# Half-tile causal diagonal in chunked attention A, with value copies moved to the DMA queue

## The chip, the cores and the metric

The kernel runs on one core of a Trainium2 chip. The metric is the device time of one execution in microseconds (us); lower is better. Three runs of the kernel before took 351.57, 351.86 and 356.25 us, so the median is 351.86 us. The engines are called PE (matmul), PEld (its weight loads), DVE (vector), ACT (activation), POOL (GpSimd) and SP (the engine whose queue issues nearly all DMAs).

## The reference, cut to what matters

Two independent attentions are computed from two inputs of 2,048 tokens by 640 columns, with 32 heads of 20 columns each, and their outputs are set side by side.

```
# A: four segments of 512 tokens, causal softmax in a segment, a memory over the earlier ones
for s in range(4):
    logits = einsum('bhqd,bhkd->bhqk', qs, ks) * scale + mask      # mask: key > query
    a_dot = einsum('bhqk,bhkd->bhqd', softmax(logits), vs)
    a_mem = (phi(qs) @ M) / (phi(qs) @ z + 1e-06)
    o = g * a_mem + (1.0 - g) * a_dot                              # g = sigmoid(beta)
    M, z = M + phi(ks).T @ vs, z + sum(phi(ks))
# B: causal attention in a sliding window of 256
mask = (i - j >= 0) & (i - j < 256)
o = softmax(where(mask, q @ k.T * scale, -1e9)) @ v
out = concatenate([A's o @ wo, B's o @ wo], axis=-1)
```

## The kernel before, in words

**Tiling.** Each attention is cut into four chunks of 512 tokens, which run alternately: A0, B0, A1, B1, A2, B2, A3, B3. The 32 heads are eight groups of four. The four heads of a group lie on partitions 0, 32, 64 and 96, so that four small matmuls run side by side on the PE. For each chunk there are projections of q and k (five pieces of 128 columns) and of v (two halves of 16 heads), then scores, exponentials, masks, products with the values ("AV"), a transpose and a division, and an output projection. Three of the eight groups of q and k get their rows through a DRAM round trip of DMAs (`regroup`, lines 393 to 414).

**Scores.** `score_batch` (line 621) fills two PSUM tiles of 1,024 columns, one for each pair of heads of a group, with keys on the partitions and queries on the columns. One ACT instruction (line 647) takes the exponential of each tile into an SBUF tile `pt`. `mask` (line 658) then zeroes what the causal rule forbids: for A always on POOL, with `affine_select` (line 682); for B on POOL, and on DVE (line 664, a product with a constant 0/1 tile) for batches made of 64 by 64 corner blocks. `batches` (line 916) lists the batches of all chunks. In A, key tile `kt` of 128 keys is scored against all queries from `128*kt` on, and the 128 by 128 block on the diagonal is then masked: 512 + 384 + 256 + 128 = 1,280 columns a head. A batch has 512 columns a head, so two groups take five batches, and a chunk takes 20.

**AV.** `av` (line 687) multiplies the values of each key tile with the `pt` columns. In the last chunk, B3, `av_tile` (line 705) does it by query tile. `norm` (line 753) turns the result into `o`: a DVE transpose (`turn`, line 748), a reciprocal, and a product on POOL (line 782). For the memory term of A it first adds epsilon (line 768, DVE). `final` (line 812) stores `o` to DRAM, loads it back transposed (`oT`, line 835, two buffers), and `final_job` (line 843) multiplies it with `wo`, a row tile of 128 tokens by ten matmuls. While scores remain these use the two PSUM banks `m`, with two DVE copies (line 891) a row tile. Once the last score batch has been issued they use the score banks `sc`, with one ACT (line 874) or DVE (line 878) copy a row tile.

**Values.** `v_job` (line 550) writes the value tiles `vA` or `vB`. For B, `v_ends` (line 583) copies pieces of them on DVE (line 601) into `vL`, `vU` and `vX`, in which the rows that a corner block doesn't use are zero.

**Order.** Nothing is scheduled by the hardware. A planner (`Flow`, line 58, and the loop in `body`, from line 1116) keeps an estimated clock for each engine while it emits instructions. It issues a score batch when its inputs and a PSUM tile should be ready, otherwise an AV group, otherwise a step of a waiting projection; output projections come last in its list. Each engine runs its own queue strictly in the order that comes out. The costs given to `on_dve`, `on_pool`, `on_act` and `on_dma` steer this order and aren't instructions.

Of the kernel before, what the change touches and what calls it, by code (L numbers as in the profile page):

```python
# [9 lines left out]
ALU = mybir.AluOpType  # L10
BF16 = mybir.dt.bfloat16
F32 = mybir.dt.float32

P = 128
# [22 lines left out]
SH = P // 2  # L37
XC = SH + L

BANKS_A = [([(0, 0, 4, 0)], [("diag", 0, 1)]),  # L40
           ([(3, 3, 1, 0), (1, 1, 3, 128)], [("diag", 0, 2)])]
HALF = (2, 2, 2)

STRETCH = 10240.0 / 3.0
IDLE = 300.0
# [139 lines left out]
class _K:  # L185
# [140 lines left out]
    def consts_ends(self):  # L326
# [11 lines left out]
        nc.gpsimd.tensor_tensor(out=ends[:], in0=cm[:, 0, :], in1=cm[:, 1, :], op=ALU.add)  # L338
        self.ends = ends

    def load_beta(self, beta):
# [208 lines left out]
    def v_job(self, n, half, w_ap, v, gate, needs):  # L550
        nc, f = self.nc, self.f
        for need in needs:
            yield need
        xT = self.xs[n]
        x0 = SH if gate else 0
        for tt in range(LT):
            yield "bank"
            ps, bi = self.bank()
            for kt in range(self.KT):
                self.wide(ps, xT[:, kt, x0 + tt * P:x0 + (tt + 1) * P],  # L560
                          w_ap[:, half, kt, :], 320, kt == 0, kt == self.KT - 1)
# [12 lines left out]
            self.close(bi, f.on_dve(402.0, f.seen))  # L574
            f.open = False
        if not gate:
            self.v_ends(n, self.chunks[n][1], half, v)
        else:
            for g in range(4 * half, 4 * half + 4):
                self.mark(f.dve + 138.0, n, "v", g)  # L580
        self.used_x(n)

    def v_ends(self, n, c, half, v):


# [4 lines left out]
        todo = []  # L590
        if half == 0 and c > 0:
            pv = self.vB[(c - 1) % 2]
            todo += [(self.vU[hi, 0:2, :], pv[hi, 2:4, :], 580.0),
                     (self.vX[lo, :], pv[lo, 0, :], 380.0)]
        todo += [(self.vL[lo, :, s], v[lo, :, s], 610.0),
                 (self.vU[hi, 2:4, s], v[hi, 0:2, s], 320.0),
                 (self.vX[hi, s], v[hi, 0, s], 430.0)]
        left = [len(todo)]
        for out, in_, ns in todo:
            def go(out=out, in_=in_, ns=ns):  # L600
                self.nc.vector.tensor_copy(out=out, in_=in_)
                t = f.on_dve(ns)
                left[0] -= 1
                if left[0] == 0:
                    for g in range(4 * half, 4 * half + 4):
                        self.mark(t, n, "v", g)
# [14 lines left out]
    def score_batch(self, n, ent, kof, q, masks):  # L621

        nc, f = self.nc, self.f
        ps = [self.ps.tile([P, 2, 512], F32, name="sc", bufs=NSC) for _ in range(2)]
        cols = 0
        for g, ref, q0, nq, c0 in ent:
            k, kc = kof(ref)
            h0, h1 = {"a": (0, P), "f": (0, P), "l": (0, SH), "u": (SH, P)}[ref[0]]
            for j in range(4):
                rows = slice(HD * j, HD * j + DH)  # L630
                nc.tensor.matmul(ps[j // 2][h0:h1, j % 2, c0:c0 + nq],  # L631
                                 lhsT=k[rows, g, kc + h0:kc + h1],
                                 rhs=q[rows, g, q0:q0 + nq],
                                 start=True, stop=True, tile_position=(HD * j, h0),
                                 skip_group_check=ref[0] in "lu")
            cols += nq
        if ent[0][1][0] in "lu":
            t = f.on_pe("row64", 40.0 * len(ent), cols / 2)
        else:
            t = f.on_pe("row", cols / 2.4 + 10.0 * len(ent), cols)  # L640
        lo = min(e[4] for e in ent)
        hi = max(e[4] + e[3] for e in ent)
        pts = []
        ready = []
        for i in range(2):
            pt, slot = self.piece("pt", NPT, 1, BF16, (P, 2, 512))
            nc.scalar.activation(out=pt[:, :, lo:hi], in_=ps[i][:, :, lo:hi], func=ACT.Exp,  # L647
                                 scale=self.scale)
            te = f.on_act(2 * (hi - lo) * 0.833 + 52.0, t)
            self.sc_free.append(te)  # L650
            for m in masks:
                ready.append(None)
                self.mask(m, pt, te, ready, len(ready) - 1)
            pts.append(pt)
            self.pt_of.setdefault(n, []).append(slot)
        return pts, ready

    def mask(self, m, pt, te, ready, x):
        nc, f = self.nc, self.f
        kind, c0, n = m  # L660
        if kind == "ends":
            def go():
                blk = pt[:].rearrange("p h (b c) -> p (h b) c", c=SH)
                nc.vector.tensor_tensor(  # L664
                    out=blk, in0=blk,
                    in1=self.ends[:].unsqueeze(1).to_broadcast([P, 1024 // SH, SH]),
                    op=ALU.mult)
                ready[x] = f.on_dve(602.0, te)
            f.at(te - 50.0, go)
            return  # L670
        if kind == "diag":
            blk = pt[:, :, c0:c0 + n * P]
            pat = [[0, 2 * n], [1, P]]
            base, mul, r = 0, -1, 2 * n * P
        else:
            blk = pt[:].rearrange("p h (b c) -> p h b c", c=2 * P)[:, :, 0:n, c0:c0 + SH]
            sign = 1 if kind == "near" else -1
            pat = [[0, 2], [0, n], [sign, SH]]
            base, mul, r = (SH, -1, 2 * n * SH) if kind == "near" else (-1, 1, 2 * n * SH)

        def select():
            nc.gpsimd.affine_select(out=blk, in_=blk, pattern=pat, compare_op=ALU.is_ge,  # L682
# [70 lines left out]
    def norm(self, turned, dst, add_to, last, g=None):  # L753
# [11 lines left out]

        def s1():
            if add_to:
                nc.vector.tensor_tensor(out=rr[:], in0=tv[:, :, DH],
                                        in1=self.eps[:, g:g + 1].to_broadcast([P, NB]),
                                        op=ALU.add)  # L770
# [145 lines left out]
    def batches(self, chunks):  # L916
# [6 lines left out]
        far = lambda n: ("far", P + SH, n)  # L923
        for n, (kind, c) in enumerate(chunks):
            if kind == "A":
                for g0 in range(0, G, 2):
                    for g in (g0, g0 + 1):
                        for ent, ms in BANKS_A:
                            out.append([n, [(g, ("a", kt), P * q0, P * nq, c0)
                                            for kt, q0, nq, c0 in ent], ms, []])  # L930
                        if g == g0:
                            kt, q0, nq = HALF
                            out.append([n, [(g0 + x, ("a", kt), P * q0, P * nq, 256 * x)
                                            for x in range(2)],
                                        [("diag", 0, 1), ("diag", 256, 1)], [g0]])
                    out[-1][3].append(g0 + 1)
                continue

            def ends(g, qt, c0):
# [76 lines left out]
    def body(self, xA, A_wq, A_wk, A_wv, A_wo, A_beta, xB, B_wqkv, B_wo, out2d):  # L1016
# [38 lines left out]
        self.vU = big.tile([P, LT, VW], BF16, name="vU")  # L1055
        self.vX = big.tile([P, VW], BF16, name="vX")
        self.vA = self.v_tile("vA")
        self.consts_mz()
        nc.vector.memset(self.vL[:].bitcast(F32), 0.0)
        self.consts_mem()  # L1060
# [165 lines left out]
    def one_group(self, n, kind, c, g, what, parts, left, o_t, groups_done, scro, wo, out2d):  # L1226
# [135 lines left out]
```

## Time and profile before

The profiled execution took 352.71 us as a whole, of which the profile's span covers 350.6 us.

| engine | busy us | share of the span | instructions |
|---|---|---|---|
| PE | 326.4 | 93% | 5617 |
| ACT | 315.0 | 90% | 358 |
| POOL | 294.3 | 84% | 592 |
| DVE | 278.2 | 79% | 557 |

| part of the span | length us | what ends it |
|---|---|---|
| first score of A0 to first score of B0 | 46.2 | from 9.3 to 55.5 us |
| A1 and A2 and A3, each to the next chunk's first score | 37.3, 36.6, 36.8 | 132.7, 213.4, 291.8 us |
| B0, B1 and B2, each to the next chunk's first score | 39.9, 44.1, 41.6 | 95.4, 176.8, 255.0 us |
| B3, first to last score | 37.8 | 329.6 us |
| rest after the last score | 21.0 | 350.6 us |

The bounds are the start times of the score matmuls on PE in the trace. Busy time counts an engine as busy while any of its instructions runs. Matmuls are pipelined, so PE's share overstates its work; the times from the start of one matmul to the start of the next tell more. The granted PE clock was 1.00 throughout.

### The profile page before, as it was taken

What the parts mean: (1) busy time and instruction counts of PE and PEld (TensorE: products, weight loads), DVE (VectorE), ACT (ScalarE), POOL (GpSimd) and SP (SyncE); (2) the same over time, 40 slices, a digit from 0 to 9 for tenths busy, and PEclk for the clock granted to TensorE, in tenths of its full rate; (3) what the DMA queues carried; (4) which work ended last, traced back from release to release, by engine and by line L of the source; (5) the groups of instructions that cost most, each with busy time, mean ns of one, the idle gap of its engine ahead of it and who ended that gap; (6) DMA issues with size and microseconds to landing.
All of it is one profiled execution on the core that took longest, in us unless ns stands there. A gap on an engine that the chain in (4) does not pass through costs nothing.

```text
span 350.6 us, 13578 instructions
## 1 busy us (share of the span) xinstructions
PE 326.4 (93%) x5617; PEld 167.0 (48%) x5617; DVE 278.2 (79%) x557; ACT 315.0 (90%) x358; POOL 294.3 (84%) x592
## 2 busy tenths in 40 slices
PE   7999999989999999999999999988999999899994
PEld 2443435444544345455644436454543445566672
DVE  5687677999958999999967998997867999766621
ACT  2897499999999999999999999999999999989831
POOL 6589388988898989999898989899988989987720
PEclk9999999999999999999999999999999999999999
DMA  7945617526675133033794025030483032675773
GB/s 233 376 159 129 165 32 227 128 64 178 200 124 123 22 77 122 2 93 69 175 193 104 0 63 155 3 79 8 82 143 77 2 75 61 146 140 150 146 183 115
DMA packets 69374, 40.54 MB, mean 116 GB/s; under 512 B 48448, under 2 KB 67520, under 8 KB 69312
## 3 DMA queue, kind: packets, MB, share of 16 engines
q1 hardware_dynamic: 67584, 38.35, 45.2%
q10 hardware_dynamic: 1728, 1.32, 1.2%
q8 instruction: 44, 0.72, 0.9%
q14 instruction: 18, 0.15, 0.1%
HBM read 16.06 MB, written 16.38 MB: 93 GB/s over the span
## 4 chain that ended last, share of the span: by engine, by line
PE 48%; DVE 22%; POOL 11%; issue 6%; ACT 5%; DMA 5%; SPq 2%; DVEq 0%; ACTq 0%; POOLq 0%
PE m L735 30%; PE sc L631 9%; POOL pt L682 7%; PE m L696 6%; ACT pt L647 5%; DVE tt L748 4%; DVE pt L664 3%; DMA xT<-in_B_x_dram 2%; PE m L717 2%; DMA scr_o<-o 2%; POOL o L782 2%; DVE kB L445 1%; PE sc L735 1%; DVE pq L471 1%; DVE qA L445 1%
## 5 line engine op out<-in xcount | busy, mean ns | idle before, releaser
L647 ACT ACTIVATE pt<-sc 128x1024 bf16<-128x1024 f32 (+1 forms) x320 | 296.6, 1070 | 14.9 <-PE sc L631 12.9
L682 POOL TENSOR_SCALAR_AFFINE_SELECT pt<-pt 128x256 bf16<-128x256 bf16 x448 | 209.6, 495 | 36.0 <-ACT pt L647 30.8
L748 DVE STREAM_TRANSPOSE tt<-m 128x512 f32<-128x512 f32 x88 | 60.7, 706 | 19.4 <-PE m L696 9.4
L782 POOL TENSOR_TENSOR o<-tt,rr 128x320 bf16<-128x320 f32 x64 | 51.2, 801 | 2.8 <-DVE rr L774 2.7
L631 PE MATMUL sc<-qB,kB 20*64 20x64 bf16 (+2 forms) x1728 | 39.0, 217 | 1.2 <-issue 0.6
L735 PEld LDWEIGHTS <-xT 128*128 128x128 bf16 x320 | 28.7, 97 | 22.4 <-issue 11.6
L735 PEld LDWEIGHTS <-oT 128*128 128x128 bf16 x320 | 28.8, 97 | 17.2 <-issue 3.5
L631 PE MATMUL sc<-qA,kA 20*128 20x128 bf16 (+3 forms) x512 | 36.1, 300 | 0.9 <-ACT pt L647 0.3
L631 PEld LDWEIGHTS <-kB 20*64 20x64 bf16 (+1 forms) x1728 | 21.7, 98 | 25.1 <-issue 23.1
L735 PE MATMUL m<-wv_A,xT 128*128 128x320 bf16 x160 | 27.4, 300 | 3.7 <-DVE kA L445 2.0
L891 DVE CAST ot<-m 128x320 bf16<-128x320 f32 x46 | 21.9, 480 | 8.5 <-PE m L735 8.3
L735 PE MATMUL m<-xT,wq_A 128*128 128x512 bf16 x100 | 26.6, 386 | 1.1 <-DVE qA L445 0.9
L664 DVE TENSOR_TENSOR pt<-pt,ends 128x1024 bf16<-128x1024 bf16 x32 | 27.6, 875 | 0.0
L735 PE MATMUL m<-xT,wk_A 128*128 128x512 bf16 x100 | 27.2, 392 | 0.3
L735 PE MATMUL m<-xT,wBq 128*128 128x512 bf16 x100 | 25.8, 380 | 1.2 <-DVE tt L748 1.2
L735 PE MATMUL m<-xT,wBk 128*128 128x512 bf16 x100 | 25.3, 381 | 0.6 <-DVE kB L445 0.6
L735 PE MATMUL m<-wBv,xT 128*128 128x320 bf16 x160 | 25.6, 300 | 0.3 <-DVE tt L748 0.2
L631 PEld LDWEIGHTS <-kA 20*128 20x128 bf16 x512 | 10.5, 91 | 30.5 <-issue 29.8
L696 PE MATMUL m<-pt,vA 128*32 128x128 bf16 (+3 forms) x512 | 24.0, 302 | 0.5 <-POOL pt L682 0.3
L735 PE MATMUL m<-wo_A,oT 128*128 128x320 bf16 x120 | 20.8, 300 | 0.2 <-DVE ot L891 0.2
L802 POOL TENSOR_TENSOR o<-o,u 128x320 bf16<-128x320 bf16 x24 | 20.5, 854 | 0.0
L445 DVE CAST qB<-m 128x512 bf16<-128x512 f32 x20 | 13.6, 682 | 7.4 <-PE m L735 7.4
(87 smaller groups left out, 427.7 us busy)
## 6 DMA issues: line engine op xcount, KB each, us to landing
scr_o<-o SPq DMA_DIRECT2D x28, 160.0 KB
out_dram<-ot SPq DMA_DIRECT2D x27, 160.0 KB
xT<-in_B_x_dram SPq DMA_DIRECT2D x4, 720.0 KB
scr_pk<-e SPq DMA_DIRECT2D x15, 128.0 KB
xT<-in_A_x_dram SPq DMA_DIRECT2D x3, 640.0 KB
scr_kA<-kA SPq DMA_DIRECT2D x16, 60.0 KB
scr_qA<-qA SPq DMA_DIRECT2D x16, 60.0 KB
kA<-scr_kA SPq DMA_DIRECT2D x16, 60.0 KB
```

The lines of the kernel that those rows point to most:

```text
L445: nc.vector.tensor_copy(out=dst[:, m, at:at + L], in_=ps[:, :])
L631: nc.tensor.matmul(ps[j // 2][h0:h1, j % 2, c0:c0 + nq], lhsT=k[rows, g, kc + h0:kc + h1], rhs=q[rows, g, q0:q0 + nq], start=True, stop=Tr ...
L647: nc.scalar.activation(out=pt[:, :, lo:hi], in_=ps[i][:, :, lo:hi], func=ACT.Exp, scale=self.scale)
L664: nc.vector.tensor_tensor(out=blk, in0=blk, in1=self.ends[:].unsqueeze(1).to_broadcast([P, 1024 // SH, SH]), op=ALU.mult)
L682: nc.gpsimd.affine_select(out=blk, in_=blk, pattern=pat, compare_op=ALU.is_ge, fill=self.zero, base=base, channel_multiplier=mul)
L696: nc.tensor.matmul(O[HD * j:HD * j + HD, q0:q0 + nq], lhsT=v[:, VS * h:VS * h + HD], rhs=pts[j // 2][:, j % 2, c0:c0 + nq], start=(n_ == 0 ...
L717: nc.tensor.matmul(O[HD * j:HD * j + HD, o0:o0 + nq], lhsT=v[:, VS * h:VS * h + HD], rhs=pts[j // 2][:, j % 2, c0:c0 + nq], start=(n_ == 0 ...
L735: self.nc.tensor.matmul(ps[:, 0:n], lhsT=lhsT, rhs=rhs, start=start, stop=stop)
L748: self.nc.vector.transpose(out=tt[:], in_=O[:, :])
L782: nc.gpsimd.tensor_tensor(out=dst, in0=a, in1=b, op=ALU.mult)
L802: nc.gpsimd.tensor_tensor(out=dst, in0=dst, in1=u[:], op=ALU.add)
L891: nc.vector.tensor_copy(out=ot[:, 320 * hf:320 * hf + 320], in_=ps[:, 0:320])
```

## The change

**Diagonal.** A key tile is now scored only from query `128*kt + 64` on: 448 + 320 + 192 + 64 = 1,024 columns a head, two batches a group. Each has one half-tile triangle at columns 0 to 63 and one at 256 to 319, masked by one `affine_select` of kind `near` for each `pt`. What is left of the diagonal is, for each key tile, the square of its first 64 keys and first 64 queries. The squares of four groups go into one batch, as 64 matmuls with 64 output rows: even key tiles on partitions 0 to 63 (`p`), odd ones on 64 to 127 (`s`). They are masked by DVE with a new constant `tri`. A chunk has 18 batches.

**Values.** AV takes the squares from a new tile `vH`: even key tiles have their first 64 rows in place, odd ones have them moved to partitions 64 to 127, and the rest is zero. Two DMAs on SP fill it for each half of an A chunk's values. The copies in `v_ends` become DMAs on SP as well.

**Epsilon.** The addition in `norm` changes from `tensor_tensor` with a broadcast operand to `tensor_scalar` with a per-partition scalar. It is still issued to DVE.

Two setup steps are added: a POOL memset of `vH`, and `tri` (a memset and two selects on POOL).

```diff
-BANKS_A = [([(0, 0, 4, 0)], [("diag", 0, 1)]),
-           ([(3, 3, 1, 0), (1, 1, 3, 128)], [("diag", 0, 2)])]
-HALF = (2, 2, 2)
+BANKS_A = [[(0, 64, 256, 0), (3, 448, 64, 256), (0, 320, 192, 320)],
+           [(1, 192, 256, 0), (2, 320, 192, 256), (1, 448, 64, 448)]]
...
+    def consts_tri(self):
...
+        nc.gpsimd.memset(self.vH[:].bitcast(F32), 0.0)
+        self.f.on_pool(1300.0)
+        self.tri = tri = cp.tile([P, SH], BF16, name="tri")
+        nc.gpsimd.memset(tri[:], 1.0)
+        for t, base in ((tri[:], SH), (tri[0:SH, :], 0)):
+            nc.gpsimd.affine_select(out=t, in_=t, pattern=[[1, SH]], compare_op=ALU.is_ge,
+                                    fill=0.0, base=base, channel_multiplier=-1)
...
-            for g in range(4 * half, 4 * half + 4):
-                self.mark(f.dve + 138.0, n, "v", g)
+            w = 16 * VS
+            s = slice(0, w) if half == 0 else slice(w, VW)
+            t = f.dve + 138.0
+
+            def go():
+                for x, rows in enumerate((slice(0, SH), slice(SH, P))):
+                    nc.sync.dma_start(out=self.vH[rows, x::2, s], in_=v[0:SH, x::2, s])
+                    tl = f.on_dma(1, 410.0, t)
+                for g in range(4 * half, 4 * half + 4):
+                    self.mark(tl, n, "v", g)
+            f.at(t, go)
...
-        for out, in_, ns in todo:
-            def go(out=out, in_=in_, ns=ns):
-                self.nc.vector.tensor_copy(out=out, in_=in_)
...
-            f.when_idle(f.dve + 138.0, go)
+        t = f.dve + 138.0
+
+        def go():
+            for out, in_, ns in todo:
+                self.nc.sync.dma_start(out=out, in_=in_)
+                tl = f.on_dma(1, ns, t)
+            for g in range(4 * half, 4 * half + 4):
+                self.mark(tl, n, "v", g)
+        f.at(t, go)
...
-        if kind == "ends":
+        if kind in ("ends", "tri"):
+            by = self.ends if kind == "ends" else self.tri
...
-                    in1=self.ends[:].unsqueeze(1).to_broadcast([P, 1024 // SH, SH]),
+                    in1=by[:].unsqueeze(1).to_broadcast([P, 1024 // SH, SH]),
...
-                nc.vector.tensor_tensor(out=rr[:], in0=tv[:, :, DH],
-                                        in1=self.eps[:, g:g + 1].to_broadcast([P, NB]),
-                                        op=ALU.add)
+                nc.vector.tensor_scalar(out=rr[:], in0=tv[:, :, DH],
+                                        scalar1=self.eps[:, g:g + 1], scalar2=None,
+                                        op0=ALU.add)
...
-                for g0 in range(0, G, 2):
-                    for g in (g0, g0 + 1):
-                        for ent, ms in BANKS_A:
-                            out.append([n, [(g, ("a", kt), P * q0, P * nq, c0)
-                                            for kt, q0, nq, c0 in ent], ms, []])
-                        if g == g0:
-                            kt, q0, nq = HALF
-                            out.append([n, [(g0 + x, ("a", kt), P * q0, P * nq, 256 * x)
-                                            for x in range(2)],
-                                        [("diag", 0, 1), ("diag", 256, 1)], [g0]])
-                    out[-1][3].append(g0 + 1)
+                for g0 in (0, 4):
+                    for x in range(4):
+                        for ent in BANKS_A:
+                            out.append([n, [(g0 + x, ("a", kt), q0, nq, c0)
+                                            for kt, q0, nq, c0 in ent], [near(2)], []])
+                        if x == (1 if n == 0 else 0):
+                            out.append([n, [(g0 + y, (("p", "s")[kt % 2], kt), P * kt, SH,
+                                             P * y + SH * (kt // 2))
+                                            for y in range(4) for kt in range(LT)],
+                                        [("tri", 0, 0)], list(range(g0, g0 + x + 1))])
+                        elif x:
+                            out[-1][3].append(g0 + x)
...
-        late = [(7600.0, self.consts_beta)]
+        late = [(7000.0, self.consts_tri), (7600.0, self.consts_beta)]
...
+            if what in "ps":
+                return self.vH[:, u, :]
```

More of the change, by code (lines that the diff above doesn't have):

```diff
@@ L339, in consts_ends @@
         self.ends = ends
+    def consts_tri(self):
+        nc, cp = self.nc, self.cp
+        nc.gpsimd.memset(self.vH[:].bitcast(F32), 0.0)
[5 more added lines that the diff above has]
+                                    fill=0.0, base=base, channel_multiplier=-1)
     def load_beta(self, beta):
@@ L589, in v_ends @@
         s = slice(0, w) if half == 0 else slice(w, VW)
-        todo = []
+        todo = [(self.vL[lo, :, s], v[lo, :, s], 820.0),
+                (self.vU[hi, 2:4, s], v[hi, 0:2, s], 410.0),
+                (self.vX[hi, s], v[hi, 0, s], 205.0)]
         if half == 0 and c > 0:
             pv = self.vB[(c - 1) % 2]
[L593 to L598, printed above, removed]
-        for out, in_, ns in todo:
-            def go(out=out, in_=in_, ns=ns):
-                self.nc.vector.tensor_copy(out=out, in_=in_)
[L602 to L606, printed above, removed]
-            f.when_idle(f.dve + 138.0, go)
+            todo += [(self.vU[hi, 0:2, :], pv[hi, 2:4, :], 820.0),
+                     (self.vX[lo, :], pv[lo, 0, :], 410.0)]
+        t = f.dve + 138.0
[6 more added lines that the diff above has]
+        f.at(t, go)
     def v_tile(self, name, now=True):
@@ L627, in score_batch @@
             k, kc = kof(ref)
-            h0, h1 = {"a": (0, P), "f": (0, P), "l": (0, SH), "u": (SH, P)}[ref[0]]
+            h0, h1 = {"a": (0, P), "f": (0, P), "l": (0, SH), "u": (SH, P), "p": (0, SH),
+                      "s": (SH, P)}[ref[0]]
+            if ref[0] == "s":
+                kc -= SH
             for j in range(4):
@@ L634, in score_batch @@
                                  start=True, stop=True, tile_position=(HD * j, h0),
-                                 skip_group_check=ref[0] in "lu")
+                                 skip_group_check=ref[0] in "lups")
             cols += nq
-        if ent[0][1][0] in "lu":
+        if ent[0][1][0] in "lups":
             t = f.on_pe("row64", 40.0 * len(ent), cols / 2)
@@ L670, in mask @@
             return
[L671 to L679, printed above, removed]
+        blk = pt[:].rearrange("p h (b c) -> p h b c", c=2 * P)[:, :, 0:n, c0:c0 + SH]
+        sign = 1 if kind == "near" else -1
+        pat = [[0, 2], [0, n], [sign, SH]]
+        base, mul, r = (SH, -1, 2 * n * SH) if kind == "near" else (-1, 1, 2 * n * SH)
         def select():
@@ L1057, in body @@
         self.vA = self.v_tile("vA")
+        self.vH = big.tile([P, LT, VW], BF16, name="vH")
         self.consts_mz()
```

## The prediction

> **What bounds the kernel now.** I read the windows by chunk first, because the busy shares of the page (PE 93%, ACT 90%) don't say which engine sets the pace of a stage. Columns: window, length, busy time and count of PE, PEld, DVE, ACT and POOL, then clock, DMA share, GB/s. Rows are B1, A2, B2, A3, B3 and the rest after the last score.
>
> ```profile
> 132.70:176.80 44.10, 41.05 (x918) 23.57 (x914) 41.73 (x81) 42.95 (x51) 42.76 (x78) 1.00 0.40 88
> 176.80:213.40 36.60, 35.62 (x452) 15.58 (x452) 30.39 (x68) 36.60 (x41) 33.67 (x63) 1.00 0.46 92
> 213.40:255.00 41.60, 38.35 (x906) 21.70 (x901) 36.10 (x68) 40.08 (x46) 38.86 (x78) 1.00 0.27 65
> 255.00:291.80 36.80, 35.77 (x453) 15.55 (x456) 30.35 (x68) 36.80 (x41) 32.91 (x63) 1.00 0.38 73
> 291.80:329.60 37.80, 35.26 (x1044) 22.46 (x1042) 26.47 (x58) 35.68 (x39) 31.95 (x70) 1.00 0.60 134
> 329.60:350.60 21.00, 15.87 (x244) 10.98 (x232) 6.72 (x13) 6.31 (x9) 5.35 (x11) 1.00 0.51 145
> ```
>
> In A2 and A3 ACT is busy for the whole window: 40 exponentials in 36.6 us, 0.915 us each. A stages are bound by ACT. B stages leave ACT 1.2 to 2.1 us idle; in B1 POOL and DVE are nearly full too. In the rest ACT does 6.3 of 21.0 us: there PE and the last transposes decide.
>
> Then the groups by form, for prices (busy us, mean ns of one; then idle before):
>
> ```profile
> L647 ACT ACTIVATE pt<-sc 128x1024 bf16<-128x1024 f32 x304 | 285.2, 1082 | 14.5 <-PE sc L631 12.5 <-POOL pt L682 0.7 <-issue 0.2
> L682 POOL TENSOR_SCALAR_AFFINE_SELECT pt<-pt 128x256 bf16<-128x256 bf16 x368 | 163.9, 472 | 27.4 <-ACT pt L647 23.1 <-PE m L735 1.8
> L682 POOL TENSOR_SCALAR_AFFINE_SELECT pt<-pt 128x512 bf16<-128x512 bf16 x64 | 42.0, 663 | 8.6 <-ACT pt L647 7.8
> L664 DVE TENSOR_TENSOR pt<-pt,ends 128x1024 bf16<-128x1024 bf16 x32 | 27.6, 875 | 0.0
> L768 DVE TENSOR_TENSOR rr<-tt,eps 128x16 f32<-128x16 f32 x24 | 7.8, 323 | 0.0
> ```
>
> Successive exponentials overlap, so I use the pace, not 1,082 ns.
>
> Last the timeline (start, length, what) for PE's own pace, from one start to the next, and for the end:
>
> ```profile
> 41.14 1.02 ACT L647 ACTIVATE pt<-sc 128x1024 bf16<-128x1024 f32 x1 [4.99 <-PE sc L631]
> 171.05 0.70 PE L631 MATMUL sc<-qB,kB 20*64 20x64 bf16 x64
> 171.69 0.72 PE L735 MATMUL m<-wo_B,oT 128*128 128x320 bf16 x4
> 185.37 0.73 PE L696 MATMUL m<-pt,vA 128*32 128x512 bf16 x16
> 186.03 0.39 PE L631 MATMUL sc<-qA,kA 20*128 20x512 bf16 x4
> 334.25 5.61 PE L735 MATMUL sc<-wo_A,oT 128*128 128x320 bf16 x40
> 339.70 4.24 PE L735 MATMUL sc<-wo_B,oT 128*128 128x320 bf16 x30
> 341.81 1.47 SPq L835 DMA_TRANSPOSE oT<-scr_o  x1
> 345.35 1.53 PE L735 MATMUL sc<-wo_B,oT 128*128 128x320 bf16 x10 [1.41 <-DMA oT<-scr_o]
> ```
>
> So 64 short score matmuls take 0.64 us (171.05 to 171.69), an A group's AV 0.66, a row tile of the output projection 5.45/4 = 1.36, one of its matmuls 0.136.
>
> **Part by part.** *ACT.* 20 batches become 18: 4 exponentials fewer a chunk, 4 x 0.915 = 3.7 us. In A1, A2 and A3 that is on the path: 11.0 us. In A0 ACT stood 4.99 us before 41.14, when 24 of 40 exponentials were done and groups 5 to 7 came out of their DMA round trip. Now 22 lie before that point and 14 after it, so 2 x 0.915 = 1.8 us is safe; the rest comes only if the round trip starts earlier. The new order does the last q piece about 1.3 us of PE work earlier. I take 3.1, with bounds 1.8 and 3.7.
>
> *PE, scores.* A batch of bulk has 512 columns as before (0.32 us, 176.71 to 177.03 in A2), now 12 matmuls for 4 or 8; A has 64 for 80 in all: -16 x 0.32 = -5.1 us. The eight batches of squares have the form of the row at 171.05: +8 x 0.64 = +5.1. Zero.
>
> *PE, AV.* 16 matmuls a group become 40, on the same 1,280 columns. A B group's AV has 52 matmuls on 1,536 columns and takes 0.84 us (177.68 to 178.52). Scaling A's 0.66 by columns gives 0.79, so 36 more matmuls cost 0.05 us, under 2 ns each. For 32 groups x 24: +1.2 us, 0.3 a chunk, in PE's slack. A rule speaks against this part: the Trainium skill, page TensorEngine Tiling (Array Packing), section Instruction Overhead, says that a matmul has some 60 cycles of overhead and that one column costs as much as 60. By it the 1,536 added matmuls, at 25 ns, would be an estimated 38 us of PE time. The row says 64 in 0.64 us, since four or eight share the array, and I go by the row.
>
> *POOL.* A's selects were 128 of 256 elements and 64 of 512; now 128 of 256: -64 x 0.663 = -42 us, 10.6 a chunk. Not on A's path, but B1 inherits a backlog from A1 (the chain of waits runs on POOL from 128.8 to 164.4 us). The memset of `vH` and the three steps for `tri` cost about 2 us (a memset of 2,048 bf16 takes 1.80, a 64-column select 0.24); POOL waits 3.86 us for its first mask at 10.82, which hides them. Uncovered they would delay that mask by 2 us.
>
> *DVE.* Off: 30 value copies, 15.0 us together. On: 16 `tri` products, 16 x 0.875 = 14.0. The epsilon step stays on DVE, whatever the change is called: between 0.323 (no gain) and 0.17 us (the 128x32 tensor_scalar of line 352), so 0 to -3.7; I take -2. The value copies go mostly from B's work; `tri` comes to A, where DVE has 6 us free.
>
> *SP.* 46 DMAs (30 in place of copies, 16 for `vH`) at 0.36 us each (four issue in 1.42): +17 us on the queue, 0.7 to 1.8 us at a place, in front of k and q stores, loads of x and stores of `o`. What waits behind them is wanted 8 us later (B1's round trip issues at 124, B1 starts at 132.7). A DVE copy of 0.25 to 0.65 us becomes issue plus landing, 2.7 us at most by SP's waits on its round trips, and up to 7.3 behind a load of x (chain, 56.30). In the new order 8 us or more of PE work lie between a half's last projection and its first AV, 4.9 in B3's second half. Cost zero; if that cover fails, at most 2 to 3 us for each of 16 halves.
>
> *The end.* In the new order output projections yield: 178 of their matmuls come after the last score, 100 before. That is 78 x 0.136 = 10.6 us more after the last score, and it takes back most of the gain. The wait of 1.6 us for the last `oT` at 343.9 is now covered (-1.6). A new wait may come: `oT` has two buffers, so chunk 6 is transposed only after chunk 4 is multiplied, and chunk 5's four row tiles (5.4 us) must cover it; issue takes 2.6 to 4.6 us and landing 2.0 (343.34 to 345.35), so 0 to 1.2 us, for chunk 5 the same. I take 0.6.
>
> *B stages.* ACT's idle time there, 1.2 to 2.1 us a stage, bounds what relief of DVE and POOL can give: 0 to 6.0 us in all. I take 1.1, B1's, where POOL had 42.76 of 44.10 us.
>
> **Sum.** Last score at 329.6 - 3.1 - 11.0 - 1.1 = 314.4. Rest 21.0 + 10.6 - 1.6 + 0.6 = 30.6. Span 345.0. Outside the span lie 352.71 - 350.6 = 2.1: 347.1. The profiled execution is 0.85 above the median, so 346.3 beside 351.86.
>
> **Rivals.** *B shrinks too.* If DVE's and POOL's queues caused all of ACT's idle time in B, another 4.9 us go: 341.4 to 344. For it: POOL 97% and DVE 95% in B1. Against: B2 and B3 have the idle time with POOL at 93% and 85%.
>
> *Nothing is left.* If PE's waits in the middle stay as they are while ACT gets its slack, A stages shorten by only some 2 us and the end still grows: 350 to 352. For it: PE has about 32 us of own work in A2's 36.6, so it is the next bound at once: 57 matmuls of 512 columns at 0.216 (15 of them start from 36.00 to 39.24), 47 of 320 at 0.136, 20 score batches at 0.32, 8 A and nearly 2 B groups of AV. Against: the new order moves 7 matmuls of output projection and 20 of B's v projection out of A2, which with the new scores makes about 29.
>
> *Slower, by short matmuls.* ACT needs 33.0 us in a new A stage, PE about 29. Its 384 added matmuls eat that slack at 10 ns each beyond their columns; at 15 ns, 4 x (384 x 0.015 - 4.0) = 7 us, the gain is gone; from 19 ns on it is over 2% slower (359). The rows give 2 ns beyond the columns in AV and 10 ns in full for squares, so this needs A's shapes to pack worse than B's.
>
> **Chances.** Forecast 0.62, B shrinks too 0.20, nothing left 0.13, slower 0.05. The range 342.5 to 351.5 takes in most of the first three. 2% (344.8 and 358.9) is about what a measurement of this kernel can tell from no change. Faster: 0.20 and 0.04 from the forecast's low edge; slower 0.05; the rest 0.71.
>
> **What would show it.** A windows of 33 us with ACT full; B windows within 1 us of before; 30 us after the last score, PE gapless but for a wait of about 1 us on `oT`; squares 0.64 us a batch; POOL near 254 us busy; no PE wait on a DMA into `vH`, `vL`, `vU`, `vX`. A shorter end, PE as the bound inside A stages, or waits on those tiles would prove me wrong.

## The result, and the profile after

| | before | changed |
|---|---|---|
| median, us | 352.74 (351.57 to 356.25) | 365.86 (362.55 to 367.75) |
| ratio, 95% interval | 1 | 1.0372 [1.0328, 1.0415] |
| profiled execution / its span, us | 352.71 / 350.6 | 367.2 / 365.5 |

Slower by 3.7%; 346.3 us was forecast. The windows by chunk of the changed kernel (window, length, busy time and count of PE, PEld, DVE, ACT and POOL, granted clock, DMA share, GB/s); the rows are A0, B1, A2, A3, B3 and the rest after the last score.

```profile
9.70:56.80 47.10, 43.09 (x714) 22.56 (x714) 32.05 (x59) 35.12 (x40) 24.62 (x57) 0.96 0.58 172
132.80:178.70 45.90, 42.62 (x938) 24.34 (x938) 39.41 (x82) 41.94 (x51) 39.84 (x75) 0.96 0.35 83
178.70:212.00 33.30, 32.18 (x789) 17.98 (x792) 27.91 (x58) 33.30 (x38) 23.96 (x50) 1.00 0.48 112
252.80:286.20 33.40, 32.74 (x744) 17.68 (x745) 27.83 (x58) 33.04 (x37) 22.66 (x46) 1.00 0.35 76
286.20:329.80 43.60, 38.33 (x1075) 24.47 (x1074) 27.97 (x62) 36.38 (x39) 32.58 (x71) 0.92 0.52 124
329.80:365.50 35.70, 26.77 (x318) 18.63 (x306) 9.49 (x16) 8.92 (x13) 4.95 (x11) 0.98 0.57 156
```

A2 and A3 last 33.3 and 33.4 us, close to the forecast (32.9 and 33.1). A0, B3 and the rest are longer than forecast by 4.0, 5.8 and 5.1 us, B0 and B1 by 2.2 and 2.9; the last score comes at 329.8 us, not 314.4. And the granted clock, 1.00 in every stage of before, is 0.92 to 0.98 in the stages that grew. From the page, the row of the clock and a queue that the prediction did not look at (packets, MB, share):

```profile
PEclk9999899989999999989999999999999998899999
...
q8 instruction: 56, 0.92, 1.1%
```

Before, the clock's row had a 9 in every slice, and q8 this row:

```profile
q8 instruction: 44, 0.72, 0.9%
```

Each packet is 16,384 bytes, and their number follows PE: 5,617 weight loads and as many matmuls before, 7,153 of each after, so 44 x 256 = 11,264 for 11,234 instructions and 56 x 256 = 14,336 for 14,306. A packet is 256 of PE's instructions. Next PE's waits, summed over the span (line, releaser: us in total, times, longest):

```profile
PE m L714 <- issue: 3.2, 2, 2.7
PE m L735 <- issue: 2.6, 2, 1.8
PE sc L753 <- DVE ot L896: 2.5, 1, 2.5
...
PE sc L652 <- issue: 2.1, 1, 2.1
...
PE sc L652 <- DMA qA<-scr_qA: 1.8, 3, 1.2
PE sc L753 <- DMA oT<-scr_o: 1.8, 1, 1.8
```

"issue" means that PE waited for nothing that the profile shows. These rows hold 7.9 us of it; before had 2.0:

```profile
PE m L717 <- issue: 1.4, 2, 1.0
PE sc L631 <- issue: 0.6, 1, 0.6
```

The timeline of PE shows where the 2.1 us lie (start, length, what, idle before):

```profile
300.48 0.71 PE L652 MATMUL sc<-qB,kB 20*64 20x64 bf16 x64
...
302.42 0.34 PE L652 MATMUL sc<-qB,kB 20*128 20x128 bf16 x12
304.83 0.23 PE L652 MATMUL sc<-qB,kB 20*128 20x128 bf16 x4 [2.06 <-issue]
```

PE stops in the middle of a batch of 16 score matmuls, after 12 of them, with their operands long there. 64 short score matmuls and 64 of an AV tile have just gone by. And here is what follows it: windows from the stop to the next, the next, and a third, chosen where the clock's records change:

```profile
302.55:305.97 3.42, 1.36 (x23) 0.84 (x16) 1.50 (x4) 1.41 (x2) 0.47 (x2) 0.99 0.54 144
305.97:309.38 3.41, 3.41 (x29) 1.62 (x26) 1.66 (x5) 3.09 (x4) 3.11 (x7) 0.51 0.15 53
316.21:319.62 3.41, 3.38 (x45) 1.88 (x46) 1.95 (x4) 1.23 (x2) 0.14 (x1) 0.51 0.19 61
```

With PE busy for 1.36 of 3.42 us, the next 3.41 us run at half clock. There are five such stretches (from 43.1, 73.8, 159.1, 305.9 and 316.2 us); at half speed each costs 3.41 x 0.5 = 1.7 us, together 8.5. Three of them (73.8, 305.9 and 316.2 us) follow stops for "issue". The one in A0 follows PE's waits for `qA` (1.8 us), and the one in B1 three waits for `vA` and POOL's masks (1.6 us), so these two are no matter of instructions. The first theory was made from these rows.

### The profile page after: what moved, and what is told of

Same layout as the page of the kernel before. It is cut to its first block, busy times and chain, and to the rows that moved or that the text cites. A ratio compares the mean times of both kernels' runs of the same rounds, so it can differ in the third digit from the quotient of the medians.

```text
span 365.5 us, 16606 instructions
## 1 busy us (share of the span) xinstructions
PE 332.0 (91%) x7153; PEld 188.6 (52%) x7153; DVE 267.7 (73%) x531; ACT 303.1 (83%) x346; POOL 255.1 (70%) x532
## 4 chain that ended last, share of the span: by engine, by line
PE 50%; DVE 14%; POOL 13%; DMA 8%; ACT 6%; issue 5%; SPq 3%; ACTq 0%; DVEq 0%; POOLq 0%
PE m L753 29%; PE sc L652 10%; POOL pt L700 8%; ACT pt L668 6%; PE m L714 6%; DVE tt L766 3%; PE sc L753 3%; POOL o L800 2%; DMA wk_A<-in_A_wk_dram 2%; DMA oT<-scr_o 2%; PE m L735 2%; DVE pt L687 2%; DMA scr_qA<-qA 2%; SPq L853 1%; DVE kA L456 1%
## 5 line engine op out<-in xcount | busy, mean ns | idle before, releaser
L668 ACT ACTIVATE pt<-sc 128x1024 bf16<-128x1024 f32 x304 | 281.9, 1049 | 28.9 <-PE sc L652 25.4
L700 POOL TENSOR_SCALAR_AFFINE_SELECT pt<-pt 128x256 bf16<-128x256 bf16 (+1 forms) x384 | 169.7, 466 | 74.9 <-ACT pt L668 73.3
L652 PE MATMUL sc<-qA,kA 20*64 20x64 bf16 (+3 forms) x1280 | 36.5, 223 | 3.3 <-DMA qA<-scr_qA 1.8
L652 PEld LDWEIGHTS <-kA 20*128 20x128 bf16 (+1 forms) x1280 | 21.3, 97 | 27.9 <-issue 24.3
L753 PE MATMUL m<-wBv,xT 128*128 128x320 bf16 x160 | 28.1, 310 | 0.6 <-DVE tt L766 0.3
L687 DVE TENSOR_TENSOR pt<-pt,ends 128x1024 bf16<-128x1024 bf16 x32 | 25.5, 815 | 0.0
L892 ACT CAST ot<-sc 128x640 bf16<-128x640 f32 x9 | 6.2, 692 | 22.7 <-PE sc L753 20.6
L714 PE MATMUL m<-pt,vA 128*32 128x256 bf16 (+2 forms) x768 | 23.8, 239 | 1.2 <-DVE vA L579 1.2
L909 DVE CAST ot<-m 128x320 bf16<-128x320 f32 x30 | 14.4, 486 | 8.6 <-PE m L753 8.4
L714 PEld LDWEIGHTS <-vA 128*32 128x32 bf16 x768 | 15.3, 97 | 9.9 <-DVE rr L790 2.1
```

The source lines that it names most:

```text
L652: nc.tensor.matmul(ps[j // 2][h0:h1, j % 2, c0:c0 + nq], lhsT=k[rows, g, kc + h0:kc + h1], rhs=q[rows, g, q0:q0 + nq], start=True, stop=Tr ...
L687: nc.vector.tensor_tensor(out=blk, in0=blk, in1=by[:].unsqueeze(1).to_broadcast([P, 1024 // SH, SH]), op=ALU.mult)
L714: nc.tensor.matmul(O[HD * j:HD * j + HD, q0:q0 + nq], lhsT=v[:, VS * h:VS * h + HD], rhs=pts[j // 2][:, j % 2, c0:c0 + nq], start=(n_ == 0 ...
L753: self.nc.tensor.matmul(ps[:, 0:n], lhsT=lhsT, rhs=rhs, start=start, stop=stop)
L892: nc.scalar.copy(out=out, in_=two[:, :, 0:320])
L909: nc.vector.tensor_copy(out=ot[:, 320 * hf:320 * hf + 320], in_=ps[:, 0:320])
```

## The experiments

Each ratio is to the kernel before, run again beside the experiment. Theories are named in the expectations as they came up.

**e1: only the count.** The kernel before with the added matmuls, and nothing else of the change.

```diff
+def cuts(ref, nq):
+    if ref != ("a", 2) or nq != 2 * P:
+        return [(0, nq)]
+    return [(32 * x, 32) for x in range(6)] + [(192, 64)]
-            for j in range(4):          # in score_batch, and likewise in av
+            for d, w in cuts(ref, nq):
+                for j in range(4):
```

> The kernel before, with one piece of A's causal diagonal (keys 256 to 383 against queries 256 to 511, 256 columns a head) issued as seven matmuls, six of 32 columns and one of 64, in the scores and in the value products: 1,536 more matmuls, as many as the change added, with the same columns, the same banks, the same exps, masks and transfers, and the same order. Theory 1 (PE's instructions come in packets of 16,384 bytes, 128 load and matmul pairs each; dense short matmuls use them up faster than they land, PE stops for 2 to 3 us with 'issue' as the reason, and the window of 3.4 us after such a stop runs at half clock): stops of over 1.5 us marked 'issue', at least one half-clock window, 355 to 366 us. Theory 2 (the value copies on SP's queue make PE wait for regroup transfers and values, and the clock falls after those waits): no half-clock window, 351 to 355 us. Theory 3 (the tail, because more output rows come after the last score): same as theory 2 here.

353.14 us, ratio 1.0076 [1.0046, 1.0106]. Its page has the 56 instruction packets of the changed kernel, and its waits this row:

```profile
PE m L724 <- issue: 1.9, 2, 1.2
```

One stretch at half clock. The count as such costs 0.0076 x 352 = 2.7 us, 1.7 ns a matmul. Theory 1 as written fell: as many packets, few stops.

**e2: fewer pieces.**

```diff
-BANKS_A = [[(0, 64, 256, 0), (3, 448, 64, 256), (0, 320, 192, 320)],
-           [(1, 192, 256, 0), (2, 320, 192, 256), (1, 448, 64, 448)]]
+BANKS_A = [[(0, 64, 448, 0), (3, 448, 64, 448)],
+           [(1, 192, 320, 0), (2, 320, 192, 320)]]
```

> The changed kernel with four full-height pieces a group in place of six (448 and 64 columns in one bank, 320 and 192 in the other; POOL masks each 64-column block by an instruction of its own, 128 more selects a kernel... 32 a chunk): 512 matmuls fewer, the same exps. Theory 1: fewer stops of PE for instructions, at most two half-clock windows, 355 to 362 us. Theories 2 and 3: no difference from the changed kernel, 362 to 368 us, as many half-clock windows as it shows.

359.82 us, 1.0251 [1.0193, 1.0310], and no half-clock stretch in its profile (span 357.7). PE still stops for "issue", 2.2 us at 301.8 and 1.1 at 312.2 among others. So the clock is not all of the loss.

**e3 and e4: the value copies.** e3 is the changed kernel with B's copies on DVE, e4 the kernel before with B's copies as transfers.

```diff
-                self.nc.vector.tensor_copy(out=out, in_=in_)     # e4; e3 the other way
+                self.nc.sync.dma_start(out=out, in_=in_)
```

> The changed kernel with B's value copies back on VectorE as before (the copies of A's values into the half-tile order stay transfers on SP). Theory 1: the stops for instructions and the half-clock windows stay (two or more), 358 to 368 us. Theory 2: the waits for regroup and value tiles go, no or one half-clock window, 348 to 356 us. Theory 3: 362 to 368 us.

> The kernel before with B's value copies as transfers on SP, and nothing else. Theory 1: no half-clock window, 350 to 354 us. Theory 2: waits for value tiles or regroup of over 1 us in the B stages, half-clock windows, 355 to 362 us. Theory 3: 350 to 354 us.

e3 368.79 us, 1.0479 [1.0419, 1.0538]; e4 354.35 us, 1.0083 [1.0050, 1.0116]. The old kernel is 2.9 us slower with the transfers, and the changed one is no better without them. Theory 2 fell as the main cause. The 2.9 us aren't all the transfers' own: e4's profile has a stop of 1.7 us for "issue" that ends at 322.6 us and a stretch at half clock from 322.5 us on.

**e5 and e6: less ScalarE, less TensorE,** each from the kernel before with the order kept.

```diff
+            if not (len(ent) == 2 and ent[0][1] == ("a", 2) and ent[0][0] >= 4):   # e5
                 nc.scalar.activation(out=pt[:, :, lo:hi], in_=ps[i][:, :, lo:hi], func=ACT.Exp,
...
+                if n > 0 and kt == self.KT - 1:                                    # e6
+                    continue
                 self.wide(ps, w_ap[:, m, kt, :], xT[:, kt, SH:XC], L,
```

> The kernel before, with four exps left out in each A chunk (two of the four batches in which two groups share a bank; the probabilities of those batches are then old data). Same order on every engine, same matmuls, same masks: 16 exps of about 1 us gone from ScalarE, nothing gone from TensorE. Theory F (the forecast's own step: an A stage lasts as long as ScalarE's exps, so four exps fewer shorten it by 3.7 us): A1 to A3 at 33 us, 337 to 342 us in all. Theory P (TensorE's own work, 313 of 351 us, is what fills the span, and an A stage was as full on TensorE, 34.7 + 2.1 us idle, as on ScalarE): A1 to A3 at 35.5 to 36.7 us, 347 to 351 us in all.

> The kernel before, with the fifth contraction step of every q and k projection from the second chunk on left out: 70 matmuls of 512 columns at about 0.213 us, 14.9 us of TensorE's work, and nothing else. Theory P: 338 to 345 us, since TensorE's work comes off until ScalarE's is the longer. Theory F: 349 to 352 us.

e5 353.36 us, 1.0006 [0.9977, 1.0035]; e6 352.73 us, 0.9980 [0.9941, 1.0019]. e5's windows for A2 and A3:

```profile
176.30:212.90 36.60, 35.56 (x455) 15.70 (x458) 30.41 (x68) 33.52 (x37) 33.95 (x64) 1.00 0.43 82
254.90:291.40 36.50, 35.54 (x453) 15.48 (x456) 30.08 (x68) 33.48 (x37) 33.02 (x63) 1.00 0.31 67
```

ACT now has 3 us free in each, and the stage is as long as before: PE is busy for 97% of it. For e5 theory F fell, and theory P's windows held; its time (347 to 351 us) was 2 us too low. In e6 ACT stays full in A3 (36.60 of 36.60 us), so nothing came off there; its 338 to 345 us were wrong.

**e12, e17 and e18: two and three engines at once.** e12 is e5 with e6. e17 leaves out selects, e18 all three.

```diff
-                                        [("diag", 0, 1), ("diag", 256, 1)], [g0]])
+                                        [("free", 0, 1), ("free", 256, 1)], [g0]])
+            if kind != "free":
                 nc.gpsimd.affine_select(out=blk, in_=blk, pattern=pat, compare_op=ALU.is_ge,
```

> The kernel before with both parts left out, the 16 exps and the 70 matmuls of the fifth contraction step, each of which alone left the time where it was. Theory B (in the A stages ScalarE and TensorE are both full, and each alone sets the stage when the other is relieved): A1 to A3 at 34 to 35.5 us, 343 to 349 us in all. If it is the order of waits and not either engine's work: 350 to 353 us, as each alone.

> The kernel before with the 16 selects a chunk of A's shared batches left out (those batches stay unmasked), some 6 to 8 us of POOL in each A stage; everything else and the order are the same. If POOL set the A stages: A1 to A3 at 33 to 35 us, 340 to 347 us in all. If it is one of several: A1 to A3 at 36 to 37 us, 350 to 354 us in all.

> The kernel before with the selects of e17 and the exps and matmuls of e12 left out. If POOL, ScalarE and TensorE together held the A stages: A1 to A3 at 32.5 to 35 us, 338 to 346 us in all. If the written order with its waits holds them: A1 to A3 at 36 to 37 us, 349 to 353 us in all.

e12 352.00 us, 0.9949 [0.9906, 0.9992]; e17 350.90 us, 0.9973 [0.9942, 1.0004]; e18 352.39 us, 0.9990 [0.9949, 1.0031]. A2 and A3 of e18:

```profile
176.80:213.20 36.40, 35.23 (x445) 15.28 (x448) 30.50 (x67) 33.58 (x37) 27.64 (x50) 1.00 0.46 93
255.10:291.40 36.30, 35.16 (x440) 15.05 (x440) 30.36 (x67) 33.50 (x37) 27.16 (x48) 1.00 0.30 68
```

ACT has 2.8 us free, POOL 9, and PE is still busy for 97%: of all the matmuls that e6 took out, only some ten lie in each A stage. So relief of ACT and POOL alone gives an A stage nothing. That PE holds it is what the busy column says; but e12's A2 is as long with PE at 94% and ACT at 92%:

```profile
175.60:212.20 36.60, 34.48 (x436) 15.24 (x441) 30.69 (x68) 33.53 (x37) 33.86 (x63) 1.00 0.46 88
```

An edit that takes much of PE's work out of an A stage and nothing else was not run, and the written order with its waits is not excluded.

**e7, e8 and e11: remedies in place.** e7 computes the first A chunk as before; e8 puts the late stores on ScalarE's queue; e11 is e2, e7 and e8 together.

```diff
-                on = "sp"                # e8, in final_job after the last score
+                on = "act"
+                if n == 0:               # e7, in batches; and no vH transfers for chunk 0
+                    for g0 in range(0, G, 2):
+                        for g in (g0, g0 + 1):
+                            for ent, ms in BANKS_0:
```

> The changed kernel with the first A chunk computed as before (20 batches of whole tiles, no half-tile copies of its values), the other three by half tiles. Theory Q (the squares of four groups in one batch need queries and keys of all four, which in the first chunk come by the regroup transfers just in time, and the first value products wait longer): A0 at 46 us with no wait of over 1 us, no half-clock window at 43 us, 358 to 362 us in all. If the first chunk is not to blame: 364 to 370 us, with four exps more.

> The changed kernel with all output stores after the last score on ScalarE's queue, where SP's stand behind DMA transposes; TensorE's order is the same. If the wait of 2.6 us in the tail for a free output tile comes from SP's queue: that wait gone, the rest after the last score 33 us, 362 to 364 us in all. If not: 365 to 367 us.

> Three remedies together: the changed kernel with the first A chunk as before, four full-height pieces a group for six, and the late output stores on ScalarE's queue. If their gains add (10, 6 and 4 us of the changed kernel's 366): 346 to 350 us, faster than the kernel before by 1 to 2%. If they share their gain, since each of them mostly removes half-clock windows and stops for instructions: 351 to 356 us.

e7 355.71 us, 1.0080 [1.0047, 1.0113]; e8 361.36 us, 1.0206 [1.0139, 1.0272]; e11 359.36 us, 1.0155 [1.0083, 1.0227], no better than e7 alone. e7's A0 is 47.7 us long, no shorter than the changed kernel's 47.1: theory Q was right that e7 gains, and wrong in its reason. e8 came out a little below its 362 to 364 us, but its A0 is 2.9 us shorter than the changed kernel's too, where the edit changes nothing. And e11 has this row among its waits of PE in B3, two stops of some 2 us that e7 does not have:

```profile
PE sc L658 <- issue: 4.2, 2, 2.4
```

The sum of remedies was no sum. What also changes from e7 to e11 is the number of PE's instructions ahead of each burst.

**Where the stops lie.** PE's rows of the trace were numbered from 0 on: each load and each matmul as one, with the few semaphore and drain rows between them (5 before, 7 to 9 in the changed kernel up to the stops). The table has the number of the last row before each stop, and the start of the packet of q8 that PE then waits for.

```
kernel    stop at us   number mod 256   length us   packet starts at us
before       305.50          192           1.27          304.09
before       319.01          192           0.87          317.26
before       326.77          192           0.55          324.46
changed       70.70          192           2.92           71.09
changed      226.18          192           0.70          224.40
changed      302.55          192           2.27          302.32
changed      314.25          192           2.00          313.58
changed      330.69          192           0.99          329.25
```

All eight lie at the same place in a block of 256, and in all eight PE goes on 1.3 to 1.6 us after the end of that packet's transfer. Over the traces of all twenty runs, with every load counted twice in place of load and matmul (some matmul rows are missing), 52 of the 53 waits for "issue" of over 0.45 us lie at 192 or 193. On a count that starts at 256 j for the j-th packet (from 0 on), no packet of the two kernels starts to move before PE stands at 175, and PE is dry at 448: some 270 instructions have to last until the packet is there. From count 176 until PE goes on, the eight took 3.8 to 7.2 us. In B3, 64 score matmuls and 64 of an AV tile are 256 instructions, and PE runs them in 1.4 us (300.48 to 301.91).

**e9, e10 and e14: the borders moved.** Tiny matmuls of zeros in idle time at the start, k = 70, 99 and 128.

```diff
+                if n == 0 and m == 1 and what == "k" and kt == 0:
+                    z = self.blk[:].rearrange("p x j c -> p (x j c)")
+                    for x in range(k):
+                        c = HD * (x % 4)
+                        nc.tensor.matmul(ps[c:c + HD, 0:HD], lhsT=z[:, 0:HD],
+                                         rhs=z[:, 0:HD], start=True, stop=True,
+                                         tile_position=(0, c), skip_group_check=True)
```

> The changed kernel with 70 tiny matmuls of zeros (128 x 32 weights, 32 columns, overwritten at once) put into TensorE's idle time at 7.7 us, where it waits for a weight: 140 instructions more, so that the borders of the 16,384-byte instruction packets (256 instructions) fall 140 instructions earlier in the program; nothing else differs. Theory S (in the traces so far TensorE stops exactly 448 instructions into a packet's count, 272 after the point at which the next packet is asked for, when those 272 run in less than the 4 to 5 us that the packet takes): the stops at 70.8, 302.7 and 314.3 us of the changed kernel (2.9, 2.2 and 2.0 us) go, smaller ones come at other places (some 62.4, 307 and 320 us on that trace's axis, 0.6 to 1.5 us each), fewer half-clock windows (at most three), 357 to 363 us. If the stops belong to the work and not to the packets: the same places, 364 to 368 us.

> As the run with 70, with 99 tiny matmuls: 198 instructions more. Theory S: the stop at 302.7 us goes, stops come at some 60.7 us (2 us), 91.5 us (1.4), 236 us (1.3), 309.8 us (1.8) and 319 us (1.1), more in sum than without (8.5 for 6.4 us by the same working), 363 to 370 us. If not: the same places as without, 365 to 369 us.

> The changed kernel with 128 tiny matmuls of zeros at 7.7 us: 256 instructions more, exactly one packet, so the borders fall at the same matmuls as in the changed kernel. Theory S: the stops at the changed kernel's 302.7 and 314.3 us are back, at the same matmuls, and the time is 361 to 368 us, with up to 1 us for the tiny matmuls themselves. If what helped was the tiny matmuls at the start and not the borders: 353 to 358 us.

e9 354.28 us, 1.0020 [0.9983, 1.0057]; e10 357.26 us, 1.0107 [1.0026, 1.0188]; e14 363.54 us, 1.0268 [1.0197, 1.0339]. With 140 instructions more, the changed kernel's median is 11.6 us lower; with 256 more, one whole packet, most of the loss is back. e9 and e14 both have tiny matmuls at the start and differ in 58 of them: 1.0020 and 1.0268, some 8.7 us, is what the place of the borders is worth here. e14's timeline stops after the twelfth matmul of the same batch, and e9's has one stop of more than 0.5 us left, elsewhere:

```profile
302.96 0.34 PE L659 MATMUL sc<-qB,kB 20*128 20x128 bf16 x12
305.49 0.23 PE L659 MATMUL sc<-qB,kB 20*128 20x128 bf16 x4 [2.18 <-issue]
```

```profile
179.14 0.21 PE L721 MATMUL m<-pt,vL 128*32 128x64 bf16 x3 [1.83 <-issue]
```

Theory S held on its main point. Its table of places was half right: the big stops of 302.7 and 314.3 us went in e9, as written, but those named in their stead did not come, and one came that was not named; e10 was 6 us faster than written. The time a packet takes is not the constant that the working took.

**e13, e15 and e16: the change again, and two counter-tests.** e13 is the changed kernel unedited, e15 is e9 with e8, e16 the kernel before with e9's 70.

> The changed kernel once more, without an edit. Theory S: the same program has the same packet borders, so the stops at 302.7 and 314.3 us come again at the same matmuls, with two to five half-clock windows, 362 to 367 us.

> The 140 instructions of e9 and the stores of e8 together. Theory S, with a tail that is a cost of its own: 350 to 353 us, one to three less than e9, no wait of over 1.5 us for an output tile in the tail. If e8's gain was only chance in the half-clock windows: as e9, 353 to 356 us.

> The kernel before with the 140 instructions of e9. By the working that fits the stops (272 instructions in less than 4.5 us) its sum of stops goes from 4.7 to 6 us: 352 to 356 us, a ratio of 1.00 to 1.01. If the tiny matmuls at the start are a gain by themselves: 340 to 349 us.

e13 364.71 us, 1.0290 [1.0227, 1.0353], with stops at the same two matmuls. e14, run beside it, is 1.2 us faster, within the intervals, so the tiny matmuls by themselves are worth little in the changed kernel. e15 353.93 us, 1.0004 [0.9966, 1.0042]: no faster than e9, so the stores of e8 are no gain that can be told here. e16 351.99 us, 0.9968 [0.9940, 0.9997]: the tiny matmuls at the start are no large gain in themselves. Of the kernels that compute everything, e16 alone has an interval below 1, by 0.3%; none that holds the change beats the kernel before.

## Why the prediction was wrong

The step that failed is the pair of terms *PE, scores* ("Zero") and *PE, AV* ("+1.2 us"): short matmuls were priced by their duration, 64 in 0.64 us, and the prediction had no term for what feeds them. In its place the runs showed PE standing still for its own instructions, 7.9 us against 2.0 before, and the half clock after three of these stops, 3 x 1.7 = 5.1 us. By these rows that is 11.0 of the 20.5 us between the profiled span (365.5) and the forecast one (345.0). Other rows hold most of what is left: two stretches at half clock after other waits (3.4 us), PE's waits for `qA` in A0 (1.8), and waits at the end (3.7 more than set). That the rows add up so was not tested one by one; the border's share was, by e9 and e14.

As a duration the row was near: e1 adds 1,536 short matmuls for 2.7 us, stops included. (The Trainium skill's 60 cycles a matmul, TensorEngine Tiling (Array Packing), section Instruction Overhead, had made an estimated 38 us; the measurement decides against it.) But their instructions come 256 at a time, and where the packets' borders fall against the bursts is worth 1.0268 against 1.0020 between two kernels that differ in 58 matmuls of nothing. The rival "slower, by short matmuls" had the sign and not the mechanism: a steady 19 ns a matmul is not there.

With most stops gone, e9 shows what the other steps were worth. Its windows for A0, B1, A2, B3 and the rest:

```profile
9.60:52.80 43.20, 40.28 (x707) 21.95 (x714) 32.14 (x59) 35.00 (x40) 24.12 (x57) 1.00 0.63 187
...
126.00:171.70 45.70, 41.89 (x932) 24.32 (x938) 39.46 (x82) 41.95 (x51) 39.98 (x75) 0.96 0.39 89
171.70:208.30 36.60, 32.94 (x780) 18.16 (x792) 27.98 (x58) 33.56 (x38) 24.38 (x50) 0.95 0.42 97
...
282.40:321.00 38.60, 35.33 (x1075) 23.36 (x1075) 27.67 (x62) 35.93 (x39) 32.28 (x71) 1.00 0.67 142
321.00:352.80 31.80, 26.44 (x322) 18.58 (x309) 9.62 (x16) 9.00 (x13) 4.96 (x11) 1.00 0.65 173
```

- *A stages.* Forecast 43.1, 33.6, 32.9 and 33.1 us; e9 43.2, 34.0, 36.6 and 33.3. The numbers hold, but for A2, which has the stop at 177 us and a half-clock window. The reason given, "A stages are bound by ACT", is not shown: in e5 four exps fewer shorten nothing. What also shrinks in an A stage of the changed kernel is PE's work: A2 has none of the output projection's matmuls, where before it had 9, and 20 of B's v projection for 40. The prediction knew of this shift, and used it against its rival "nothing is left" alone. Which relief shortens the stage, ACT's or PE's, no run separates, so it is open how far these good numbers are luck.
- *B stages.* Forecast 39.9, 43.0, 41.6 and 37.8; e9 39.2, 45.7, 40.8 and 38.6. B1's 2.7 us too many hold a half-clock window (1.7 us), which here too follows waits for `vA` and POOL's masks and not a stop.
- *The end.* Forecast 30.6 us; e9 31.8, the changed kernel 35.7. The 10.6 us for the moved projections were right: 178 of their matmuls stand after the last score. The wait taken off at 1.6 us has 1.41 in its row. The new wait for `oT` took 1.8 us where 0.6 were set, and a wait that the prediction did not have is in the timeline of the changed kernel:

```profile
348.13 5.16 SPq L853 DMA_TRANSPOSE oT<-scr_o  x4
...
353.39 6.35 SPq L924 DMA_DIRECT2D out_dram<-ot  x4
...
357.83 1.56 DVE L896 CAST ot<-sc 128x640 bf16<-128x640 f32 x2 [6.15 <-DMA out_dram<-ot]
358.71 1.52 PE L753 MATMUL sc<-wo_B,oT 128*128 128x320 bf16 x10 [2.46 <-DVE ot L896]
```

SP issues four transposes for 5.2 us; the output stores behind them start late, no output tile is free for DVE, and PE waits 2.5 us. In e9, with the same queue, that wait isn't there.

- *SP.* "Cost zero": as forecast, the changed kernel's profile has no wait of PE on a transfer into `vH`, `vL`, `vU` or `vX`. e4 is 2.9 us slower for B's part, and has 1.7 us at half clock and 3.6 us of "issue" (2.0 before); what the transfers cost besides is not shown.
- *POOL* 255.1 us busy for 254 forecast. *DVE* 267.7: the 16 `tri` products took 10.3 us, not 14.0. The epsilon step gave nothing:

```profile
L687 DVE TENSOR_TENSOR pt<-pt,tri 128x1024 bf16<-128x1024 bf16 x16 | 10.3, 675 | 0.0
...
L786 DVE TENSOR_SCALAR rr<-tt,eps 128x16 f32<-128x16 f32 x24 | 7.8, 324 | 0.0
```

324 ns for 323 before, the end of the range that says no gain, not the 2 us taken.

e9's span is 352.8 us for 345.0 forecast. A2 accounts for 3.7 of the 7.8, B1 for 2.7, the rest for 1.2. Whether a kernel without any stop would reach 345 was not tried. Open too: why A0 took 47.1 us in the profiled execution of the change, with a wait of 1.8 us on the regroup transfers (48.3 in e13, with the same wait). The tiny matmuls needn't be the reason that it took 43.2 to 44.5 in e9 and e14: in e8, which is the changed kernel up to the last score, A0 took 44.2 us, without that wait. And open is how much of e2, e3, e7 and e11 is their edit and how much the borders that it moved.

## What to carry to other kernels

Price a burst of short matmuls by its instructions too: count loads and matmuls, and ask whether some 270 of them can pass before the next packet of 256 arrives (3.8 to 7.2 us at the stops here). Two kernels that differ in their number of PE instructions differ in where the borders fall, so measure each at several borders (a few dummy matmuls in idle time do it) before an edit is called good or bad. An engine that is busy for a whole stage need not be the one that sets it: take work away from it alone, and see.

## What the runs showed of the hardware

- PE's instructions arrive in packets of 16,384 bytes on a DMA queue of their own. PE stopped at a count of 192 modulo 256 in all eight stops of the table, for 0.55 to 2.92 us, and went on 1.3 to 1.6 us after the end of the next packet's transfer.
- The packets share the DMA engines with the data. Ahead of the stop at 70.7 us PE passed the place from which on packets were seen to start (175 into the block) at 66.4 us, and the packet began to move at 71.1; a load of weights, a load of x and the value copies had been issued from 60.1 to 66.3 us, and the DMA engines were over 90% busy from 67.5 us on. From 300.5 us on the same took 1.8 us.
- A gap of about 2 us was enough for half clock in the next window of 3.41 us (302.6 and 305.9 us); in B1 of the changed kernel three gaps of 0.45 to 0.63 us were, and in e1 one of 1.2 us (half clock from 310.7 us on). It was not always so: e14 has a stop of 2.2 us at 303 and no half clock in B3. The Trainium skill, TensorE: Matmul & The Clock Gate, section Why this matters for your kernels, asks for no gaps over some 3 us; here shorter ones did it. Its window length, 3,413 ns (Part 1: The HAM clock gate), agrees with the trace.
